# U and the read-out computed transposed, with two heads in two column halves, in an RWKV-7 plus SoLU kernel

## The chip, the cores and the metric

One core of one Trainium2 chip runs the whole program. The metric is the device time of one execution in microseconds (us); several runs are summed up by their median. Below, PE is TensorE (PEld its weight loads), DVE is VectorE, ACT is ScalarE, POOL is GpSimd, and SP is SyncE, which here only issues transfers.

## The reference, cut to what matters

A recurrence over 768 steps for 4 batches of 8 heads with 40 channels each, and behind it a two-layer MLP over the 3072 tokens:

```python
for t in range(S):
    y[:, :, t] = einsum('bhd,bhde->bhe', r_t, state)
    Sa = einsum('bhde,bhe->bhd', state, a_t)
    state = state * w_t[:, :, None, :] - einsum('bhd,bhe->bhde', Sa, b_t) \
            + einsum('bhd,bhe->bhde', v_t, k_t)
x = y.transpose(0, 2, 1, 3).reshape(3072, 320)
h = x @ w_in                       # 320 -> 1024
solu = h * softmax(h)
ln = (solu - mean) / sqrt(var + 1e-6) * g_ln
out = ln @ w_out                   # 1024 -> 320
```

All data are 32-bit floats, except the three MLP weights, which arrive as 64-bit floats and are narrowed on DVE.

## The kernel before

Time is cut into 6 chunks of 128 steps, which gives N = 24 (chunk, batch) pairs; a pass `i` handles one pair, with the batches in turn. `front(i)` (six passes ahead) makes the decay factors: `decay` takes the logarithm of `w`, sums it along time with products against constant triangles (`pcum`) and takes exponentials (`inv`, `ex`); POOL scales `k`, `b` and `a` with them (`kb`, `ah`), and PE transposes `ah` and `b` (`paT`, `pbT`) and multiplies them to the triangular matrix `nt`. `invert(n)` inverts the 32x32 diagonal blocks of four passes on DVE, and `solve` joins them to the inverse of the 128x128 triangle, `tinvT`, with small products (`py`, `pz`; 32x32 and 64x64). Results of `front` pass through DRAM (`aT_dram`, `kb_dram`, `nt_dram`) and come back by `bring(i)` as `aTx`, `kbx`, `ntx`. `attend` makes the masked score matrices `psi` and `lamv` (one 128x128 matrix for each head). `recurrence` forms `x0`, then U by eight products with `tinvT` (`pu`), the new state (`pst`), and the masked scores `lamu` from U transposed (`pnuT`). `readout` adds up y in `pyo`, scales it with `ex` into `x`, and transposes it into `xT` (`pxT`). `mlp(i - 2)` makes `h`, the softmax and the normalisation, transposes (`plnT`) and multiplies with the second weight (`po`).

The main loop writes a pass in two halves, each with `in_turn`, which takes one step of each part by turns: first `attend(i+1)`, `recurrence(i)` and `front(i+6)`, then `solve(i+1)`, `readout(i)` and `mlp(i-2)`. A scheduler orders the instructions of each engine from that; every engine, and SP's queue of transfers, runs its list strictly in order. A 32-bit matrix product in the source is two MATMUL instructions with a weight load each in the trace; a transpose is one. The read-out's products are

```python
for h in range(H):
    for j, lam in enumerate((d["lamv"], d["lamu"])):
        nc.tensor.matmul(t[:, h * D:h * D + D], lhsT=lam[:, h % 2, h // 2, :], rhs=kb[:, j, h, 0:D], ...)
```

that is, 128x128 weights are loaded for each and 40 columns stream through them.

Of the kernel before, what the change touches and what calls it, by code (L numbers as in the profile page):

```python
# [17 lines left out]
Q = 32  # L18
GRP = 4
# [32 lines left out]
def kernel(  # L52
# [28 lines left out]
    NK = -(-DM // P)  # L81
# [35 lines left out]
    ah_t = zeroed("ah", [P, H, 64], 2)  # L117
# [7 lines left out]
    x_t = zeroed("x", [P, NK * P], 2)  # L125
    y_mid = const.tile([P, 2, G, Q], FP32, name="y_mid")
    y_last = const.tile([P, 2, G, 64], FP32, name="y_last")
    w_in = zeroed("w_in", [P, NK, DFF], 1)[0]
# [32 lines left out]
    def load_weight(dst, src):  # L161

        if src.dtype == FP32:
            nc.scalar.dma_start(out=dst, in_=src)
            yield
            return
        n, width = src.shape
        for lo in range(0, width, 128):
            hi = min(width, lo + 128)
            bits = two.tile([P, 128], I64, tag="bits", name="bits")[0:n, 0:hi - lo]  # L170
            nc.scalar.dma_start(out=bits, in_=src[:, lo:hi])
            narrow(dst[:, lo:hi], bits)
            yield

    def weights():
        nc.scalar.dma_start(out=g_rows, in_=moe_g_ln.rearrange("(c p) -> c p", p=P))
        for kt in range(NK):
            n = min(P, DM - kt * P)
            yield from load_weight(w_in[0:n, kt, :], moe_w_in[kt * P:kt * P + n, :])
# [3 lines left out]
        for c in range(NF):  # L183
            yield from load_weight(w2[:, c, :], moe_w_out[c * P:(c + 1) * P, :])
# [3 lines left out]
    def rows(p):  # L188
        return slice(64 * p, 64 * p + 64)
# [16 lines left out]
    def scores(name, lhs, rhs, dst):  # L206

        for p in range(2):
            t = bank("p" + name)
            for g in range(G):  # L210
                nc.tensor.matmul(t[:, g * P:(g + 1) * P], lhsT=lhs[rows(p), g, :],  # L211
                                 rhs=rhs[rows(p), g, :], start=True, stop=True)
# [14 lines left out]
    def load(i, late=False):  # L227
# [13 lines left out]
        for n, ap in (("w", w), ("k", k), ("b", b), ("a", a)):  # L241
            d["raw_" + n] = raw.tile([P, H, D], FP32, tag="raw_" + n, name="raw_" + n)
            nc.sync.dma_start(out=d["raw_" + n], in_=src(ap))

    def decay(i):

        d = st[i]
        lw, kb, ah = lw_t[i % 2], kb_t[i % 2], ah_t[i % 2]
# [7 lines left out]
        t = bank("pcum")  # L256
# [8 lines left out]
        f = ex[:, DM:].rearrange("p (g f c) -> p g f c", g=G, f=2)  # L265
        d["to_mid"] = f[:, :, 1, :]
        d["to_end"] = small.tile([P, G, 2], FP32, tag="to_end", name="to_end", bufs=AHEAD + 1)
        nc.gpsimd.tensor_tensor(out=d["to_end"], in0=f[:, :, 0, :],
                                in1=c_("diag").rearrange("p (g c) -> p g c", c=2), op=ALU.mult)
        d["ah"] = ah  # L270

# [8 lines left out]
    def front(i):  # L280
# [12 lines left out]
        scores("nt", bT, aT, nt)  # L293
# [41 lines left out]
    def bring(i):  # L335
# [13 lines left out]
        d["aT"] = two.tile([P, G, P], FP32, tag="aTx", name="aTx")  # L349
        nc.sync.dma_start(out=d["aT"], in_=d["aT_dram"])  # L350
# [62 lines left out]
    def recurrence(i):  # L413
# [14 lines left out]
        x0 = two.tile([P, DM], FP32, tag="x0", name="x0")  # L428
        nc.scalar.copy(out=x0, in_=t[:, 0:DM])
# [177 lines left out]
```

## Time and profile before

| what | value |
|---|---|
| median of 3 runs | 1231.67 us (1228.69 to 1231.69) |
| the profiled execution's own time | 1226.91 us |
| its span, from first to last instruction | 1225.1 us |
| PE busy | 1111.7 us, 91% of the span |
| DVE, ACT, POOL busy | 522.2, 261.1, 133.2 us |
| mean granted clock of PE | 0.791 of full speed |

The stages below are cut where the first product `px` of `recurrence` starts in pass 0, pass 3 and pass 23 (157.4, 289.4 and 1158.2 us). The profiled execution took 1.8 us more than its span and 4.8 us less than the median. The clock that the profile shows for PE has two levels, 1.2 and 2.4 GHz; a mean of 0.50 over a stretch says that all of it ran at the lower one, 1.00 that all ran at the higher. An instruction's duration includes its way through the array, so neighbours overlap; the pace of a group is read from the chain of waits, where a group's time over its count is the step from one to the next.

### The profile page before, as it was taken

The page shows a single profiled execution, that of the slowest core. Times are in us where ns is not written, and L with a number is a line of the kernel's source. Part 1 is how long each engine was busy: PE and PEld are TensorE (multiplying, and loading weights), DVE is VectorE, ACT ScalarE, POOL GpSimd, SP SyncE. Part 2 cuts the span into 40 slices and gives each one's busy share as a digit, 9 for nine tenths or more (in the row PEclk, how much of TensorE's full clock was granted, in tenths as well). Part 3 has the DMA queues.
Part 4 walks back from the last instruction along what each step waited for, and adds up shares of the span by engine and source line. Part 5 has one row for each costly group of instructions (what it writes and reads, how often), then busy time and mean ns, then how long its engine had stood idle before and what let it go on. Part 6 is the DMA issues. An engine that isn't in the chain of part 4 may idle for free.

```text
span 1225.1 us, 20360 instructions
## 1 busy us (share of the span) xinstructions
PE 1111.7 (91%) x8281; PEld 904.7 (74%) x8281; DVE 522.2 (43%) x1466; ACT 261.1 (21%) x549; POOL 133.2 (11%) x182
## 2 busy tenths in 40 slices
PE   1753499999899999999999999999999999999986
PEld 1642397888698878788788788788788778788763
DVE  5779932275223373132552242562233743331222
ACT  1211021123123212122212122222222212122111
POOL 6210013001011001011001011001101000000000
PEclk9855566588689877789768789889888888788777
DMA  9656542443343333253234243235223122210000
GB/s 158 151 125 167 141 99 73 103 90 109 64 102 87 83 82 99 57 115 88 72 83 104 60 113 89 71 83 132 76 54 94 33 74 60 47 36 6 6 6 11
DMA packets 275740, 101.22 MB, mean 83 GB/s; under 512 B 250680, under 2 KB 259392, under 8 KB 275648
## 3 DMA queue, kind: packets, MB, share of 16 engines
q1 hardware_dynamic: 269088, 94.41, 33.1%
q10 hardware_dynamic: 6560, 5.52, 1.7%
q8 instruction: 65, 1.06, 0.4%
q14 instruction: 27, 0.22, 0.1%
HBM read 62.14 MB, written 37.75 MB: 82 GB/s over the span
## 4 chain that ended last, share of the span: by engine, by line
PE 85%; DVE 7%; DMA 3%; issue 2%; ACT 1%; POOL 1%; SPq 0%; POOLq 0%; DVEq 0%; ACTq 0%
PE h L489 15%; PE pyo L469 9%; PE po L526 9%; PE pz L380 4%; PE pu L433 4%; PE pst L441 4%; PE plamv L211 4%; PE px L426 3%; PE py L400 3%; PE pz L407 3%; PE ppsi L211 3%; PE plamu L211 3%; PE pnt L211 2%; PE plnT L521 2%; PE py L380 2%
## 5 line engine op out<-in xcount | busy, mean ns | idle before, releaser
L489 PE MATMUL h<-w_in,xT 128*128 128x512 f32 x288 | 205.5, 838 | 7.8 <-DVE c L508 7.8
L526 PE MATMUL po<-w,lnT 128*128 128x320 f32 x384 | 110.5, 442 | 0.0
L526 PEld LDWEIGHTS po<-w,lnT 128*128 128x128 f32 x384 | 75.3, 197 | 40.8 <-issue 8.0
L489 PEld LDWEIGHTS h<-w_in,xT 128*128 128x128 f32 x288 | 67.0, 265 | 51.7 <-issue 49.0
L213 DVE TENSOR_TENSOR psi<-ppsi,cst 128x512 f32<-128x512 f32 x48 | 31.5, 686 | 172.9 <-PE ppsi L211 172.9
L469 PE MATMUL pyo<-kbx,lamu 128*128 128x40 f32 x384 | 92.2, 331 | 0.0
L469 PE MATMUL pyo<-kbx,lamv 128*128 128x40 f32 x384 | 89.3, 323 | 0.0
L469 PEld LDWEIGHTS pyo<-kbx,lamu 128*128 128x128 f32 x384 | 75.2, 243 | 1.0 <-issue 1.0
L469 PEld LDWEIGHTS pyo<-kbx,lamv 128*128 128x128 f32 x384 | 72.7, 236 | 0.2
L493 DVE TENSOR_REDUCE nmax<-h 128x1 f32<-128x1024 f32 x24 | 29.4, 1224 | 90.5 <-PE h L489 90.5
L211 PE MATMUL pnt<-aT,bT 64*128 64x128 f32 x384 | 52.0, 335 | 16.9 <-ACT bT L203 16.9
L324 DVE TENSOR_TENSOR u<-u,prod 128x30 f32<-128x30 f32 (+9 forms) x180 | 60.2, 335 | 4.0
L473 DVE TENSOR_TENSOR x<-pyo,ex 128x320 f32<-128x320 f32 x24 | 11.8, 492 | 117.5 <-PE pyo L469 117.5
L322 DVE TENSOR_TENSOR prod<-blk,u 128x30 f32<-128x30 f32 (+9 forms) x180 | 60.0, 334 | 4.2
L409 DVE TENSOR_SCALAR tinvT<-pz 64x256 f32<-64x256 f32 x48 | 19.9, 416 | 96.7 <-PE pz L407 96.2
L511 POOL TENSOR_TENSOR rs<-c,mhalf 128x1 f32<-128x1 f32 x24 | 13.4, 560 | 436.2 <-DVE c L510 397.5
L211 PEld LDWEIGHTS pnt<-aT,bT 64*128 64x128 f32 x384 | 46.7, 233 | 19.2 <-ACT bT L203 19.2
L380 PE MATMUL py<-tinv,ntx 32*32 32x32 f32 x768 | 27.8, 196 | 34.9 <-DMA tinv<-ut_dram 34.9
L213 DVE TENSOR_TENSOR lamv<-plamv,cst 128x512 f32<-128x512 f32 x48 | 31.7, 687 | 64.7 <-PE plamv L211 64.7
L400 PEld LDWEIGHTS py<-tinv,ntx 64*64 64x64 f32 x384 | 39.7, 206 | 24.8 <-issue 18.3
L211 PEld LDWEIGHTS plamu<-rT,nuT 64*128 64x128 f32 x384 | 39.5, 200 | 21.9 <-ACT nuT L203 21.9
L263 POOL TENSOR_TENSOR kb<-raw_k,inv 128x320 f32<-128x320 f32 x24 | 20.9, 871 | 319.8 <-ACT inv L255 303.5
(122 smaller groups left out, 2011.8 us busy)
## 6 DMA issues: line engine op xcount, KB each, us to landing
kb_dram<-kb SPq DMA_DIRECT2D x24, 512.0 KB, 3.3
kbx<-kb_dram SPq DMA_DIRECT2D x24, 512.0 KB, 4.0
aT_dram<-aT SPq DMA_DIRECT2D x24, 256.0 KB, 2.3
aTx<-aT_dram SPq DMA_DIRECT2D x24, 256.0 KB, 3.0
nt_dram<-nt SPq DMA_DIRECT2D x24, 192.0 KB, 2.8
ntx<-nt_dram SPq DMA_DIRECT2D x24, 192.0 KB, 3.0
raw_w<-in_w_dram SPq DMA_DIRECT2D x24, 160.0 KB, 3.5
raw_k<-in_k_dram SPq DMA_DIRECT2D x24, 160.0 KB, 3.6
```

The source lines that it names most:

```text
L211: nc.tensor.matmul(t[:, g * P:(g + 1) * P], lhsT=lhs[rows(p), g, :], rhs=rhs[rows(p), g, :], start=True, stop=True)
L213: nc.vector.tensor_tensor(out=dst[:, p], in0=t.rearrange("q (g c) -> q g c", g=G), in1=tri.unsqueeze(1).to_broadcast([P, G, P]), op=ALU.mult)
L322: nc.vector.tensor_tensor(out=t, in0=nb[:, j:j + 1, j + 1:Q].to_broadcast([P, j, m]), in1=u[:, 0:j, j:j + 1].to_broadcast([P, j, m]), op=A ...
L324: nc.vector.tensor_tensor(out=u[:, 0:j, j + 1:Q], in0=u[:, 0:j, j + 1:Q], in1=t, op=ALU.subtract)
L380: nc.tensor.matmul(t[quarter(out), c:c + Q], lhsT=lhs(p, g), rhs=rhs(p, g), start=True, stop=True)
L400: nc.tensor.matmul(t[hi, g * 64:g * 64 + 64], lhsT=nt[lo, G * p + g, 32:96], rhs=tinv[lo, p, g, :], start=True, stop=True)
L407: nc.tensor.matmul(t[lo, g * 64:g * 64 + 64], lhsT=y_last[hi, p, g, :], rhs=tinvT[hi, p, g, hi], start=True, stop=True)
L433: nc.tensor.matmul(t[:, h * D:h * D + D], lhsT=d["tinvT"][:, h % 2, h // 2, :], rhs=x0[:, h * D:h * D + D], start=True, stop=True)
L441: nc.tensor.matmul(t[:, g * 80:g * 80 + 80], lhsT=pair(kb[:, j], g), rhs=x[:, 2 * g:2 * g + 2, 0:D], start=j == 0, stop=j == 1)
L469: nc.tensor.matmul(t[:, h * D:h * D + D], lhsT=lam[:, h % 2, h // 2, :], rhs=kb[:, j, h, 0:D], start=not ci and h == 0 and j == 0, stop=j ...
L489: nc.tensor.matmul(h[:, hh], lhsT=d["xT"][:, kt, :], rhs=w_in[:, kt, hh], start=kt == 0, stop=kt == NK - 1)
L526: nc.tensor.matmul(o[:, 0:DM], lhsT=lnT[:, f, :], rhs=w2[:, f, :], start=f == 0, stop=f == NF - 1)
```

## The change

- **U transposed.** `pu` swaps its operands: `x0` of a head (128x64, padded) is loaded as weights and `tinvT` of the head (128 columns) streams. Even heads write output partitions 0 to 63, odd heads 64 to 127 of the same bank. The result is U transposed (`nuT`) at once; U itself comes from four transposes back (`pnu`).
- **Read-out transposed.** `pyo` swaps its operands in the same way: `kb` of a head (128x64) is loaded, the score matrix (128 columns) streams, two heads in two column halves. y comes out as channels by time; DVE scales it with the factors `exT` (128x512 instead of 128x320), and four transfers from SBUF to SBUF pack 40 of each 64 rows into `xT`. The three transposes `pxT` and the ACT copy behind them are gone.
- **Factors transposed.** `decay` makes the factors for `a` transposed (`pcx`: 4 products with 132 columns, two exponentials) instead of one product with 320 columns and four with 4; `a` is transposed raw and scaled by DVE out of PSUM (`ax`), so that POOL's `ah` and ACT's copy of `aT` are gone. `ax` with the factors (520 KB) goes through DRAM instead of `aT` (256 KB); `to_end` is made in `bring`.
- **MLP split.** `mlp` becomes `hidden` (up to the normalised `ln`), written beside `recurrence` in the first half of a pass, and `output` in the second.
- **Weights.** `w_in` is cut into tiles of 3, 3 and 2 heads, so that each block of its narrowing is fetched by three (two) transfers on ACT's queue instead of one; the zero fill of `w_in` on POOL is gone.

```diff
-        ex = d["ex"] = two.tile([P, DM + 16], FP32, tag="ex", name="ex", bufs=AHEAD + 1)
+        ax = d["ax"] = two.tile([P, G, AXW], FP32, tag="ax", name="ax")
...
-        nc.tensor.matmul(t[:, 0:DM], lhsT=c_("cum_ex"), rhs=lw[:, :, 0:D], start=True, stop=True)
-        for g in range(G):
-            nc.tensor.matmul(t[:, DM + 4 * g:DM + 4 * g + 4], lhsT=pair(lw, g), rhs=c_("half"),
-                             start=True, stop=True)
-        nc.scalar.activation(out=ex, in_=t[:, 0:DM + 16], func=AF.Exp)
+        for j in range(2):
+            t = bank("pcx")
+            for g in range(2):
+                nc.tensor.matmul(t[:, g * 132:g * 132 + 132], lhsT=pair(lw, 2 * j + g), rhs=cst[:, lo:lo + 132],
+                                 start=True, stop=True)
+            nc.scalar.activation(out=ax[:, 2 * j:2 * j + 2, P:], in_=t[:, 0:264].rearrange("p (g t) -> p g t", g=2),
+                                 func=AF.Exp)
...
-        nc.gpsimd.tensor_tensor(out=ah[:, :, 0:D], in0=d["raw_a"], in1=heads(ex[:, 0:DM]), op=ALU.mult)
...
-        aT = transposed("aT", d["ah"], "aT", 2)
+        t = bank("paT")
+        for g in range(G):
+            nc.tensor.transpose(out=t[:, g * P:(g + 1) * P], in_=pair(d["a"], g), identity=ident)
+        nc.vector.tensor_tensor(out=ax[:, :, 0:P], in0=t.rearrange("p (g t) -> p g t", g=G), in1=ax[:, :, P:2 * P],
+                                op=ALU.mult)
...
         t = bank("pu")
         for h in range(H):
-            nc.tensor.matmul(t[:, h * D:h * D + D], lhsT=d["tinvT"][:, h % 2, h // 2, :],
-                             rhs=x0[:, h * D:h * D + D], start=True, stop=True)
-        nc.scalar.mul(out=nu[:, :, 0:D], in_=heads(t[:, 0:DM]), mul=-1.0)
+            nc.tensor.matmul(t[half(h % 2), h // 2 * P:h // 2 * P + P], lhsT=x0[:, h, :],
+                             rhs=d["tinvT"][:, h % 2, h // 2, :], start=True, stop=True)
+        nuT = two.tile([P, G, P], FP32, tag="nuT", name="nuT")
+        nc.scalar.mul(out=nuT.rearrange("p g t -> p (g t)"), in_=t, mul=-1.0)
+        yield
+        t = bank("pnu")
+        for g in range(G):
+            nc.tensor.transpose(out=t[:, g * P:(g + 1) * P], in_=nuT[:, g, :], identity=ident)
+        nc.scalar.copy(out=nu.rearrange("p h c -> p (h c)"), in_=t)
...
-                nc.tensor.matmul(t[:, h * D:h * D + D], lhsT=lam[:, h % 2, h // 2, :], rhs=kb[:, j, h, 0:D],
-                                 start=not ci and h == 0 and j == 0, stop=j == 1, skip_group_check=True)
+                nc.tensor.matmul(t[half(h % 2), h // 2 * P:h // 2 * P + P], lhsT=kb[:, j, h, :],
+                                 rhs=lam[:, h % 2, h // 2, :], start=not ci and h < 2 and j == 0, stop=j == 1,
+                                 skip_group_check=True)
...
-        x = x_t[i % 2]
-        nc.vector.tensor_tensor(out=x[:, 0:DM], in0=t[:, 0:DM], in1=d["ex"][:, 0:DM], op=ALU.mult)
-        yield
-        t = bank("pxT")
-        for kt in range(NK):
-            nc.tensor.transpose(out=t[:, kt * P:(kt + 1) * P], in_=x[:, kt * P:(kt + 1) * P], identity=ident)
-        d["xT"] = two.tile([P, NK, P], FP32, tag="xT", name="xT", bufs=LAG + 2)
-        nc.scalar.copy(out=d["xT"].rearrange("p k t -> p (k t)"), in_=t[:, 0:NK * P])
+        x = two.tile([P, G, P], FP32, tag="x", name="x")
+        nc.vector.tensor_tensor(out=x, in0=t.rearrange("p (g t) -> p g t", g=G), in1=d["exT"], op=ALU.mult)
+        xT = d["xT"] = two.tile([P, NK, P], FP32, tag="xT", name="xT", bufs=LAG + 1)
+        for p in range(2):
+            nc.sync.dma_start(out=xT[p * D:p * D + D], in_=x[64 * p:64 * p + D, 0:3, :])
+            nc.sync.dma_start(out=xT[2 * D:3 * D, p, :], in_=x[64 * p:64 * p + D, 3, :])
...
-        in_turn(*([attend(i + 1)] if more else []), *([recurrence(i)] if i < N else []), ...
-                *([some(ws, 4, 3)] if i < LAG else []))
+        in_turn(*([attend(i + 1)] if more else []), *([recurrence(i)] if i < N else []), ...
+                *([hidden(i - LAG)] if i >= LAG else []), *([some(ws, 4, 3)] if i < LAG else []))
...
-                *([mlp(i - LAG)] if i >= LAG else []), *([some(inv, 8)] if inv else []),
+                *([output(i - LAG)] if i >= LAG else []), *([some(inv, 8)] if inv else []),
```

The scheduler moves more than the diff shows. On PE, from the end of the read-out of a middle pass to the start of the next pass's first transposes, before:

```order
L469 MATMUL pyo<-kbx,lamu 128x40
L489 MATMUL h<-w_in_128,xT 128x512
L380 MATMUL pz<-tinvT_92,y_mid 32x32 x16
L380 MATMUL pz<-y_mid,tinvT_92 32x32 x8
L400 MATMUL py<-tinv_96,ntx 64x64 x8
L477 MATMUL pxT<-cst,x_124 128x128 x3
L407 MATMUL pz<-tinvT_92,y_last 64x64 x8
L489 MATMUL h<-w_in_128,xT 128x512 x4
L521 MATMUL plnT<-cst,e 128x128 x8
L489 MATMUL h<-w_in_128,xT 128x512
L526 MATMUL po<-w_130,lnT 128x320 x8
L201 MATMUL pkT<-cst,kbx 128x128 x4
```

and the same place of the change:

```order
L485 MATMUL pyo<-lamu,kbx 64x128
L540 MATMUL plnT<-cst,e 128x128 x8
L392 MATMUL pz<-tinvT_94,y_mid 32x32 x16
L392 MATMUL pz<-y_mid,tinvT_94 32x32 x8
L545 MATMUL po<-w_129,lnT 128x320 x8
L412 MATMUL py<-tinv_98,ntx 64x64 x8
L504 MATMUL h<-w_in,xT 128x512
L419 MATMUL pz<-tinvT_94,y_last 64x64 x8
L504 MATMUL h<-w_in,xT 128x512 x2
L206 MATMUL pkT<-cst,kbx 128x128 x4
```

`po` moved from right ahead of `pkT` to the middle of the small products, and `plnT`, which needs DVE's finished `e`, right behind the read-out. On SP, whose list holds all transfers of the main loop, the place of the load of `kbx` (the next pass's `k` and `b`, which `pkT` reads first) in a middle pass, before:

```order
L300 DMA blk_dram<-nt 32x8x32 x4
L304 DMA nt_dram<-nt 512x1x96
L304 DMA nt_dram<-nt 256x1x32
L347 DMA tinvT_94<-u_dram 32x8x32 x3
L350 DMA aTx<-aT_dram 128x512
L352 DMA kbx<-kb_dram 128x1024
L239 DMA rv_104<-in_r_dram 128x8x40
L530 DMA out_dram<-osb 128x320
```

and in the change (the first two rows stand there twice, once for each half of the heads):

```order
L493 DMA xT<-x 40x384
L494 DMA xT<-x 40x128
L356 DMA axx<-ax_dram 128x1040
L549 DMA out_dram<-osb 128x320
L364 DMA kbx<-kb_dram 128x1024
L350 DMA ntx<-nt_dram 64x768
```

The load of `kbx` now stands behind the four transfers that pack y, and in 9 of the 15 passes from 3 to 17, as here, behind the store of the output, which waits for `po` and its copy `osb`; in 3 of these 9 four or more transfers of `tinvT` and `tinv` stand ahead of it as well. On DVE, between the maximum of `h` (`nmax`) and the end of the normalisation (the last row, which `plnT` needs), in a middle pass of the change:

```order
L508 TENSOR_REDUCE nmax<-h 128x1
L218 TENSOR_TENSOR lamv<-plamv,cst 128x512 x2
L513 TENSOR_TENSOR e<-h,e 128x1024
L218 TENSOR_TENSOR lamu<-plamu,cst 128x512 x2
L218 TENSOR_TENSOR nt<-pnt,cst 128x512
L517 BN_STATS bs<-e 128x6
...
L466 TENSOR_TENSOR tot<-pst,sm_120 128x320
...
L468 TENSOR_TENSOR st_116<-tot,to_end 128x8x40
L525 TENSOR_TENSOR c_5738<-c_5738,mv 128x1
L528 TENSOR_SCALAR e<-e,mv,rs 128x1024
L490 TENSOR_TENSOR x<-pyo,axx 128x512
```

The masks `lamv`, `lamu` and `nt` (a second row each of `nt` and `bs` and four small rows are left out) now stand among the MLP's steps; in many passes before, the steps of the MLP stood behind them.

## Rows read from the trace of the kernel before

**Rows 1.** The page's parts 1 and 4: busy times, and the chain by engine.

```profile
PE 1111.7 (91%) x8281; PEld 904.7 (74%) x8281; DVE 522.2 (43%) x1466; ACT 261.1 (21%) x549; POOL 133.2 (11%) x182
...
PE 85%; DVE 7%; DMA 3%; issue 2%; ACT 1%; POOL 1%; SPq 0%; POOLq 0%; DVEq 0%; ACTq 0%
```

**Rows 2.** Windows by stage: length, busy of each engine, PEclk, DMA share, GB/s.

```profile
0.00:157.40 157.40, 71.99 (x384) 61.71 (x385) 123.32 (x595) 21.47 (x43) 35.66 (x53) 0.66 0.68 148
157.40:289.40 132.00, 128.14 (x938) 110.60 (x937) 55.51 (x133) 26.49 (x59) 19.25 (x24) 0.69 0.36 85
289.40:1158.20 868.80, 861.18 (x6758) 697.06 (x6757) 326.61 (x711) 202.11 (x428) 76.69 (x102) 0.83 0.32 76
1158.20:1225.10 66.90, 50.37 (x206) 35.30 (x204) 16.73 (x30) 10.98 (x21) 1.64 (x3) 0.80 0.03 10
```

**Rows 3.** Windows, `pyo` alone: length, PE, PEld, DVE, PEclk, DMA share, GB/s.

```profile
307.50:321.10 13.60, 4.67 (x23) 4.52 (x22) 0.49 (x1) 0.50 0.28 47
399.70:403.10 3.40, 3.40 (x34) 3.40 (x32) 0.00 (x0) 1.00 0.45 83
403.10:413.40 10.30, 1.44 (x8) 1.29 (x7) 0.49 (x1) 0.50 0.48 133
...
1133.60:1140.40 6.80, 4.28 (x21) 4.13 (x20) 0.49 (x1) 0.50 0.00 0
```

**Rows 4.** The chain at full clock: start us, us, what, and how many.

```profile
413.30 1.12 PE pz L407 x16
...
415.45 0.86 PE h L489 x2
...
420.62 0.44 PE pkT L201 x4
...
425.15 0.54 PE pcum L257 x2
425.69 0.79 PE pcum L259 x8
...
428.11 1.91 PE pu L433 x16
...
440.01 1.05 PE pyo L464 x8
441.06 3.89 PE pyo L469 x32
```

**Rows 5.** Timeline of PE, products over 64 rows: start us, us, what.

```profile
395.49 1.38 PE L211 MATMUL plamu<-rT,nuT 64*128 64x128 f32 x13
396.60 0.37 PE L211 MATMUL pnt<-aT,bT 64*128 64x128 f32 x1
...
396.93 0.27 PE L211 MATMUL plamu<-rT,nuT 64*128 64x128 f32 x1
```

**Rows 6.** Timeline of PE and its weight loads in the read-out.

```profile
400.22 0.35 PE L469 MATMUL pyo<-kbx,lamv 128*128 128x40 f32 x2
400.37 0.30 PEld L469 LDWEIGHTS pyo<-kbx,lamu 128*128 128x128 f32 x2
```

**Rows 7.** The page's part 6: a DMA issue, KB, median us to landing.

```profile
kbx<-kb_dram SPq DMA_DIRECT2D x24, 512.0 KB, 4.0
```

**Rows 8.** Timeline of SP: the issue of that load in one pass.

```profile
404.57 0.35 SPq L352 DMA_DIRECT2D kbx<-kb_dram  x1
```

**Rows 9.** SP's own waits from 200 to 1100 us: total, times, longest.

```profile
SPq L530 <- ACT osb L528: 174.4, 16, 18.0
```

**Rows 10.** Waits over the whole span: us in total, times, longest.

```profile
DVE n_man L149 <- DMA bits<-in_moe_w_in_dram: 15.8, 9, 5.1
...
PE plnT L521 <- DVE e L513: 7.6, 2, 7.1
...
DVE w_in L159 <- POOL w_in L98: 7.0, 1, 7.0
```

**Rows 11.** The page's part 5, a mask on DVE.

```profile
L213 DVE TENSOR_TENSOR psi<-ppsi,cst 128x512 f32<-128x512 f32 x48 | 31.5, 686 | 172.9 <-PE ppsi L211 172.9
```

More of the change, by code (lines that the diff above doesn't have):

```diff
@@ L18 @@
 Q = 32
+TILE_HEADS = ((0, 1, 6), (2, 3, 7), (4, 5))
 GRP = 4
@@ L124 @@
     sm_t = zeroed("sm", [P, G, 2, 64], 2)
-    x_t = zeroed("x", [P, NK * P], 2)
+    x0_t = zeroed("x0", [P, H, 64], 2)
     y_mid = const.tile([P, 2, G, Q], FP32, name="y_mid")
     y_last = const.tile([P, 2, G, 64], FP32, name="y_last")
-    w_in = zeroed("w_in", [P, NK, DFF], 1)[0]
+    AXW = 2 * P + 4
+    w_in = const.tile([P, NK, DFF], FP32, name="w_in")
     w2 = const.tile([P, NF, DM], FP32, name="w2")
@@ L159, in narrow, with load_weight @@
         nc.vector.tensor_tensor(out=dst, in0=frac, in1=scale.bitcast(FP32), op=ALU.mult)
-    def load_weight(dst, src):
-        if src.dtype == FP32:
-            nc.scalar.dma_start(out=dst, in_=src)
-            yield
-            return
-        n, width = src.shape
+    def load_weight(dst, parts):
+        n, width = dst.shape
+        wide_ = parts[0].dtype != FP32
         for lo in range(0, width, 128):
             hi = min(width, lo + 128)
-            bits = two.tile([P, 128], I64, tag="bits", name="bits")[0:n, 0:hi - lo]
-            nc.scalar.dma_start(out=bits, in_=src[:, lo:hi])
-            narrow(dst[:, lo:hi], bits)
+            to = dst[:, lo:hi]
+            if wide_:
+                to = two.tile([P, 128], I64, tag="bits", name="bits")[0:n, 0:hi - lo]
+            row = 0
+            for part in parts:
+                nc.scalar.dma_start(out=to[row:row + part.shape[0]], in_=part[:, lo:hi])
+                row += part.shape[0]
+            if wide_:
+                narrow(dst[:, lo:hi], to)
             yield
@@ L177, in weights @@
         for kt in range(NK):
-            n = min(P, DM - kt * P)
-            yield from load_weight(w_in[0:n, kt, :], moe_w_in[kt * P:kt * P + n, :])
+            yield from load_weight(w_in[0:D * len(TILE_HEADS[kt]), kt, :],
+                                   [moe_w_in[h * D:h * D + D, :] for h in TILE_HEADS[kt]])
         pg = bank("pg")
@@ L183, in weights, with half @@
         for c in range(NF):
-            yield from load_weight(w2[:, c, :], moe_w_out[c * P:(c + 1) * P, :])
+            yield from load_weight(w2[:, c, :], [moe_w_out[c * P:(c + 1) * P, :]])
             nc.gpsimd.tensor_scalar(out=w2[:, c], in0=w2[:, c], scalar1=g_col[:, c:c + 1],
                                     scalar2=None, op0=ALU.mult)
-    def rows(p):
+    def half(p):
         return slice(64 * p, 64 * p + 64)
@@ L210, in scores @@
             for g in range(G):
-                nc.tensor.matmul(t[:, g * P:(g + 1) * P], lhsT=lhs[rows(p), g, :],
-                                 rhs=rhs[rows(p), g, :], start=True, stop=True)
+                nc.tensor.matmul(t[:, g * P:(g + 1) * P], lhsT=lhs[half(p), g, :],
+                                 rhs=rhs[half(p), g, 0:P], start=True, stop=True)
             nc.vector.tensor_tensor(
@@ L255, in decay @@
         nc.scalar.activation(out=inv, in_=t[:, 0:DM], func=AF.Exp)
-        t = bank("pcum")
-        nc.tensor.matmul(t[:, 0:DM], lhsT=c_("cum_ex"), rhs=lw[:, :, 0:D], start=True, stop=True)
-        for g in range(G):
-            nc.tensor.matmul(t[:, DM + 4 * g:DM + 4 * g + 4], lhsT=pair(lw, g), rhs=c_("half"),
-                             start=True, stop=True)
-        nc.scalar.activation(out=ex, in_=t[:, 0:DM + 16], func=AF.Exp)
+        lo = where["cum_ex"][0]
+        for j in range(2):
[5 more added lines that the diff above has]
+                                 func=AF.Exp)
         for j, n in enumerate("kb"):
             nc.gpsimd.tensor_tensor(out=kb[:, j, :, 0:D], in0=d["raw_" + n], in1=heads(inv), op=ALU.mult)
-        nc.gpsimd.tensor_tensor(out=ah[:, :, 0:D], in0=d["raw_a"], in1=heads(ex[:, 0:DM]), op=ALU.mult)
[L265 to L270, printed above, removed]
     def quarter(q):
@@ L348, in bring @@
                               in_=u[homes(i, q)].rearrange("h s t -> s h t"))
-        d["aT"] = two.tile([P, G, P], FP32, tag="aTx", name="aTx")
-        nc.sync.dma_start(out=d["aT"], in_=d["aT_dram"])
+        ax = d["ax"] = two.tile([P, G, AXW], FP32, tag="axx", name="axx")
+        nc.sync.dma_start(out=ax, in_=d["ax_dram"])
+        d["aT"], d["exT"] = ax[:, :, 0:P], ax[:, :, P:2 * P]
+        f = ax[:, :, 2 * P:].rearrange("p g (f c) -> p g f c", f=2)
+        d["to_mid"] = f[:, :, 1, :]
+        d["to_end"] = small.tile([P, G, 2], FP32, tag="to_end", name="to_end")
+        nc.gpsimd.tensor_tensor(out=d["to_end"], in0=f[:, :, 0, :],
+                                in1=c_("diag").rearrange("p (g c) -> p g c", c=2), op=ALU.mult)
         d["kb"] = two.tile([P, 2, H, 64], FP32, tag="kbx", name="kbx")
@@ L427, in recurrence @@
                              start=not ci and h == 0, stop=True, skip_group_check=True)
-        x0 = two.tile([P, DM], FP32, tag="x0", name="x0")
-        nc.scalar.copy(out=x0, in_=t[:, 0:DM])
+        x0 = x0_t[i % 2]
+        nc.scalar.copy(out=x0[:, :, 0:D], in_=heads(t[:, 0:DM]))
         yield
@@ L488, in mlp @@
             for kt in range(NK):
-                nc.tensor.matmul(h[:, hh], lhsT=d["xT"][:, kt, :], rhs=w_in[:, kt, hh],
+                n = len(TILE_HEADS[kt]) * D
+                nc.tensor.matmul(h[:, hh], lhsT=d["xT"][0:n, kt, :], rhs=w_in[0:n, kt, hh],
                                  start=kt == 0, stop=kt == NK - 1)
-        yield
+            yield
         nmax = small.tile([P, 1], FP32, tag="nmax", name="nmax")
@@ L511, in mlp, with output @@
         nc.gpsimd.tensor_tensor(out=rs, in0=c2, in1=mhalf, op=ALU.pow)
-        ln = q
+        ln = d["ln"] = q
         nc.vector.tensor_scalar(out=ln, in0=q, scalar1=mv[:, 0:1], scalar2=rs, op0=ALU.subtract, op1=ALU.mult)
         yield
-        yield
+    def output(i):
+        d = st[i]
+        bi, ci = where_(i)
+        ln = d["ln"]
         lnT = two.tile([P, NF, P], FP32, tag="lnT", name="lnT", bufs=1)
```

29 lines of the change are left out of this document (14 added, 15 removed).

## The prediction

> **What bounds the kernel now.** I read the shares of the engines and the chain first: PE is busy for 91% of the span and carries 85% of the chain; no other engine reaches half [rows 1]. So PE's own time counts, not that of POOL, ACT or DVE, as long as they keep ahead. Then the windows by stage [rows 2]. Until the first `px` at 157.4 us PE is busy for 72 us and DVE for 123 (it narrows weights): DVE bounds that stage. In the three passes after it, in the 20 passes from 289.4 to 1158.2 and in most of the tail PE bounds; in the 20 passes it is busy for 861.2 of 868.8 us, so a pass takes 43.4 us and PE hardly waits.
>
> But the granted clock of that stage is 0.83 of full: with two levels, 34% of its time runs at half clock. The windows around the read-out say where [rows 3]: from 399.7 to 403.1 us the clock is 1.00 and PE does nothing but `pyo`; then it is 0.50 for 10.3 us, into the small products behind. Read in this way, 20 of the 27 stretches at half clock that begin from 289.4 to 1158.2 us begin while the read-out's products run or within 0.5 us of their end; the first and the last of the 27 are shown. The read-out is also PE's longest piece of small products in a pass: 32 of them in 3.89 us, a pace of 0.12 us for 40 columns, where a transpose of 128 columns paces at 0.11 [rows 4]. So the 128x128 weight load sets the pace and the array idles between; this is the work behind which the clock falls.
>
> **The change part by part**, per pass, at full clock. A pass of 43.4 us at 0.83 is 36.1 us at full clock (a half-clock microsecond counts half).
>
> *Read-out and U.* 32 and 16 instructions remain, now with 128 columns streaming and half the weights. No row shows two column halves of one bank with all 128 rows. Bounds: with no overlap they stream at 0.11 us each, 3.52 and 1.76 us; with the halves fully side by side, one step more than half the count, 17 and 9 steps, 1.87 and 0.99. The nearest row is the score products over 64 rows, where two row halves alternate: the first `pnt` starts at 396.60 while `plamu` of the other half still starts products until 396.93 [rows 5], so queued work of two halves does run side by side. I take the second: 3.89 to 1.87 and 1.91 to 0.99, together -2.94 (with no overlap -0.52).
>
> *Product with the state.* 8 instructions, 1.05 us; with 128 columns 8 x 0.11 = 0.88: -0.17. *`pxT`*: three transposes, -0.33. *Factors*: `pcum` of L257 and L259, 0.54 + 0.79, become 8 instructions of 132 columns, 0.88: -0.45 [rows 4]. U's four transposes remain. Sum: -3.89, to 32.2 us; without overlap -1.47, to 34.6.
>
> *DVE* gets `ax` (0.69, as a mask [rows 11]) and a wider `x`, about 0.9 us on the 16.3 that it works in a pass (326.6 over 20 [rows 2]); it stays far below PE. ACT loses two copies and gets an exponential, POOL loses `ah`: hidden behind PE, at nothing; if the cover were gone, ACT's 10.1 us and POOL's 3.8 a pass would still fit three times over.
>
> *Changes of shape.* Two more stretches of half-width products make four more switches of PE's shape a pass. A switch can cost between nothing and the 0.27 us that a product takes to run through [rows 5], so 0 to 1.1; I take 0.3, since the chain shows no gap at the switches that are there. The Trainium skill (TensorEngine Tiling (Array Packing), Key Properties) says that a change of tiling mode drains the engine, which speaks against this change; it gives no price, and by the upper bound above the sum would be 0.8 a pass higher.
>
> *`kbx` on SP.* Its load is now queued behind the packing of y and, in 9 of 15 passes, behind the store of the output. SP already spends its longest waits on that store, 174 us in 16 waits [rows 9], but elsewhere. From the end of `po` to `pkT` PE has two small groups of 1.12 and two or three `h` products of 0.86 [rows 4], 4.0 to 4.8 us. The load needs `po`'s copy (at most a mask's 0.69), two issues of 0.35 and 4.0 to land [rows 7, 8, 11]: 5.4. So PE waits 0.6 to 1.4 us in six of the 15, some 2 us more in the three with `tinvT` and `tinv` ahead, and `pvT`, `prT`, `px` and all else of PE queue behind it: on average 0.9 to 1.3 over 15; I take 1.0.
>
> *The MLP's split.* `plnT` waited for DVE only twice [rows 10]. Now six masks and the state's two sums stand among the MLP's steps on DVE, and `plnT` directly behind `pyo`. Bound: nothing to six masks, 4.1 us; I take 0.5, since about ten PE groups lie between `nmax` and `plnT`.
>
> *The clock.* With 128 columns streaming, the read-out has the density of the stretch from `po` to `psi`, behind which the clock did not fall. Bounds: all falls go (0 us), or one of 10.3 us stays in each pass (5.2 lost). I take a fall in every sixth pass, 0.8, from the waits above and the INV work on DVE.
>
> A pass: 32.2 + 0.3 + 1.0 + 0.5 + 0.8 = 34.8, 20 passes 696 (before 868.8). The first three: 132 at 0.69 is 91 at full clock, less 3 x 3.9 is 79; DVE still narrows there and the clock has to come back, the upper bound is 132 - 12 = 120; I take 100. Start: 157, bounds 150 to 167: DVE no longer waits 7.0 us for the zero fill [rows 10], but three transfers instead of one feed each of 16 blocks (two for 8 more); DVE already waited for the single ones. Tail: 66.9 at 0.80 is 53.5 at best; I take 58. Span 157 + 100 + 696 + 58 = 1011. The profiled execution lies 1.8 above its span and 4.8 below the median, so the forecast is **1018 us**, its own range 975 to 1060.
>
> **Rivals.**
> - *No overlap of the column halves* (0.13). For it: no row shows them. Clock back, but 2.4 more a pass; DVE then has time, -0.5: 1018 + 20 x 1.9 + 3 x 2.4 = 1063.
> - *Load and product in turn* (0.04). If half-width loads could not run behind a product in the same rows, an instruction would cost its 0.11 and about 0.055 of load: 48 x 0.165 = 7.9 against 2.86, +5.1 a pass: 1018 + 23 x 5.1 - 10 = 1125. Against it: a load starts at 400.37 while the products of the head before, over the same 128 rows, run until 400.57 [rows 6]. The Trainium skill (TensorE: Matmul & The Clock Gate, Part 3, The mechanism) states just this rule, that loads overlap products in flight only in other row groups; this trace disagrees, by that pace of 0.12.
> - *The clock goes on falling in every pass* (0.13), since the small products behind stay: a loss of 5.2 to 6.8 (half of 10.3 and 13.6 [rows 3]) instead of 0.8, 20 x 4.4 to 6.0 and about 10 in the first passes: 1115 to 1148, say 1130.
> - *`kbx` late in every pass* (0.07): 3.4 instead of 1.0, 1018 + 20 x 2.4 = 1066, and 1100 where the clock falls on the wait.
> - *Slower* (0.04): `po` and `h` no longer stand in one dense piece; in the trace the clock rises where they do. If it stays low, a pass of 34.0 us of work takes 34.0 / (1 - s/2) with a share s at half clock; it passes 43.4 at s = 0.43 (now 0.34), and at 0.6 takes 48.6: 1018 + 20 x 13.8 = 1294.
> - *No effect* (0.01): the gain in PE turns into other waits of the same size, 1225 to 1235.
>
> **How the numbers follow.** The forecast has 0.58. The range that should hold 8 in 10 leaves out the slower case, no effect, the upper half of the falling clock, half of the loads in turn and the forecast's own low end, where every unknown term is zero (below 955): **955 to 1125**. A measurement here can tell about 0.3%. Only the last two rivals are not faster: faster 0.95, same 0.01, slower 0.04.
>
> **What the new profile would show.** Right: PEclk of the passes above 0.95; no fall behind `pyo`; `pyo`'s 32 products in 1.9 us and `pu`'s 16 in 1.0; PE still over 90% busy; passes of some 35 us. Wrong, and where: 3.5 us for `pyo` means no overlap, 5 us loads in turn; PEclk near 0.83 means that the small products hold the clock down; waits of PE `pkT` for `kbx` or of `plnT` for DVE above 1 us a pass mean that the order on SP or DVE bounds; a start above 170 us means the split fetch of `w_in`.

## The result and the profile after

The changed kernel takes 1007.04 us (1005.14 to 1008.71, 4 runs), a ratio of 0.8176 to the kernel before with an interval of 0.8151 to 0.8201; 1018 was forecast. The profiled execution took 1006.36 us, with a span of 1004.5. Executions over 1.5% longer than the fastest of the same kernel count in no ratio below, among them one of run 3 that took 1488.9 us at a mean granted clock of 0.605.

Parts 1 and 4 of the page of the changed kernel answer to [rows 1]:

```profile
PE 879.2 (88%) x8161; PEld 699.6 (70%) x8161; DVE 534.6 (53%) x1490; ACT 248.3 (25%) x525; POOL 108.1 (11%) x157
...
PE 79%; DVE 9%; DMA 7%; issue 2%; SPq 1%; ACT 0%; ACTq 0%; POOLq 0%; DVEq 0%
```

The windows by stage of the changed kernel, cut at the first `px` of passes 0, 3 and 23 like [rows 2] (length, busy time and count of PE, PEld, DVE, ACT and POOL, PEclk, DMA share, GB/s):

```profile
0.00:151.90 151.90, 61.00 (x372) 53.13 (x373) 126.50 (x594) 19.43 (x42) 27.70 (x42) 0.69 0.70 166
151.90:260.60 108.70, 99.95 (x932) 77.18 (x932) 60.26 (x151) 25.51 (x57) 18.23 (x21) 0.88 0.55 136
260.60:945.90 685.30, 674.66 (x6653) 541.42 (x6651) 330.63 (x716) 193.00 (x409) 60.53 (x91) 0.99 0.44 113
945.90:1004.50 58.60, 43.60 (x209) 27.83 (x208) 17.18 (x32) 10.40 (x19) 1.64 (x3) 0.91 0.03 12
```

The span is 220.6 us shorter: 5.5 in the start, 23.3 in the first three passes, 183.5 in the 20 passes, 8.3 in the tail. A pass went from 43.4 to 34.3 us. If a microsecond at half clock counts half, the clock cost 868.8 x (1 - 0.83) = 148 us in the 20 passes before and 685.3 x (1 - 0.99) = 7 now: some 141 of the 183.5 us. Part of the work loses less than half at half clock, by about 0.4 us a pass (shown below), so an estimate is 133 us from the clock and the other 50, 2.5 a pass, from less work on PE.

The chain through one pass at full clock (start us, us, what, count):

```profile
529.33 0.89 PE pyo L481 x8
530.22 1.95 PE pyo L485 x32
532.17 1.02 PE plnT L540 x8
533.19 1.43 PE pz L392 x48
534.62 4.50 PE po L545 x16
539.13 1.07 PE py L412 x16
...
548.78 0.90 PE pcx L267 x8
...
551.32 1.02 PE pu L445 x16
552.34 0.59 PE paT L289 x4
552.93 0.44 PE pbT L206 x4
...
556.73 0.59 PE pnu L452 x4
```

Against [rows 4] the read-out's 32 products fell from 3.89 to 1.95 us and U's 16 from 1.91 to 1.02: their two column halves run side by side. `paT` and `pnu`, groups of four transposes like `pbT`, take 0.15 us more than it: they stand directly behind products in halves.

PE's waits in the 20 passes, and DVE's for weights in the start (us in total, times, longest), which answer to [rows 10]; `issue` says that the profile names nothing that PE waited for:

```profile
PE h L504 <- issue: 6.6, 2, 3.9
PE pkT L206 <- DMA kbx<-kb_dram: 3.9, 3, 2.0
```

```profile
DVE n_man L151 <- DMA bits<-in_moe_w_in_dram: 15.3, 7, 8.1
DVE n_man L151 <- DMA bits<-in_moe_w_out_dram: 4.7, 5, 1.2
```

Two falls of the clock are left in the 20 passes, where there were 27, and each begins during one of PE's two waits in front of `h`. The second, in the chain, on DVE's timeline and in the window behind:

```profile
395.99 2.79 PE h L504 x6
398.78 3.85 issue
402.62 5.18 PE h L504 x6
```

```profile
401.30 1.22 DVE L513 TENSOR_TENSOR e<-h,e 128x1024 f32<-128x1024 f32 x1 [1.27 <-ACT e L511]
```

```profile
400.60:407.40 6.80, 4.78 (x6) 2.06 (x7) 3.76 (x8) 0.66 (x2) 0.55 (x1) 0.50 0.48 131
```

`h` has one buffer in PSUM, the memory that PE writes to. The next pass's `h` starts at 402.62, as DVE's product `e`, which reads the last one, ends (401.30 + 1.22); meanwhile PE stands still, and at 400.6 the clock falls. The first wait reads the same: `e` ends at 360.31 and `h` starts at 360.41. That `h` waits for its buffer is read from these times. PE's two longer waits for `kbx`, of 1.7 and 2.0 us, were not followed by a fall.

### The profile page after: what moved, and what is told of

Same layout as the page of the kernel before. It is cut to its first block, busy times and chain, and to the rows that moved or that the text cites. A ratio compares the mean times of both kernels' runs of the same rounds, so it can differ in the third digit from the quotient of the medians.

```text
span 1004.5 us, 20445 instructions
## 1 busy us (share of the span) xinstructions
PE 879.2 (88%) x8161; PEld 699.6 (70%) x8161; DVE 534.6 (53%) x1490; ACT 248.3 (25%) x525; POOL 108.1 (11%) x157
## 4 chain that ended last, share of the span: by engine, by line
PE 79%; DVE 9%; DMA 7%; issue 2%; SPq 1%; ACT 0%; ACTq 0%; POOLq 0%; DVEq 0%
PE h L504 13%; PE po L545 11%; PE pyo L485 5%; PE px L438 4%; PE pst L461 4%; PE plamv L216 4%; PE ppsi L216 4%; PE plamu L216 3%; PE pz L392 3%; PE pnt L216 3%; DMA kbx<-kb_dram 3%; DMA bits<-in_moe_w_in_dram 3%; PE plnT L540 3%; PE pu L445 2%; PE py L392 2%
## 5 line engine op out<-in xcount | busy, mean ns | idle before, releaser
L504 PE MATMUL h<-w_in,xT 120*128 120x512 f32 (+1 forms) x288 | 157.2, 666 | 18.2 <-issue 18.2
L504 PEld LDWEIGHTS h<-w_in,xT 120*128 120x128 f32 (+1 forms) x288 | 52.5, 205 | 61.7 <-issue 58.1
L216 PE MATMUL pnt<-ax,bT 64*128 64x128 f32 x384 | 46.8, 311 | 27.1 <-ACT bT L208 14.6
L216 PEld LDWEIGHTS pnt<-ax,bT 64*128 64x128 f32 x384 | 41.8, 210 | 28.7 <-ACT bT L208 28.7
L438 PE MATMUL px<-rv,psi 128*128 128x40 f32 x384 | 47.4, 285 | 0.0
L438 PEld LDWEIGHTS px<-rv,psi 128*128 128x128 f32 x384 | 46.5, 198 | 0.0
L216 PEld LDWEIGHTS plamv<-rT,vT 64*128 64x128 f32 x384 | 37.9, 193 | 9.2 <-issue 8.4
L216 PE MATMUL plamv<-rT,vT 64*128 64x128 f32 x384 | 42.6, 291 | 0.0
L216 PE MATMUL ppsi<-axx,kT 64*128 64x128 f32 x384 | 42.4, 291 | 0.0
L511 ACT ACTIVATE e<-h,nmax 128x1024 f32<-128x1024 f32 x24 | 26.9, 1121 | 62.4 <-DVE nmax L508 62.4
```

Source lines behind the costliest of these rows:

```text
L216: nc.tensor.matmul(t[:, g * P:(g + 1) * P], lhsT=lhs[half(p), g, :], rhs=rhs[half(p), g, 0:P], start=True, stop=True)
L438: nc.tensor.matmul(t[:, h * D:h * D + D], lhsT=d["psi"][:, h % 2, h // 2, :], rhs=vb[:, h, 0:D], start=not ci and h == 0, stop=True, skip_ ...
L504: nc.tensor.matmul(h[:, hh], lhsT=d["xT"][0:n, kt, :], rhs=w_in[0:n, kt, hh], start=kt == 0, stop=kt == NK - 1)
```

## The experiments

The theory at the outset was that of the prediction: halves that alternate run side by side, and the clock came back because the read-out streams 128 columns instead of 40. The main rival: it came back because the split put `plnT` and `po` behind the read-out. Each ratio here is to the kernel before as measured again beside the run (medians of 1224.5 us for runs 1 to 4, 1221.7 for 5 to 8 and 1222.3 for 9 to 12), so it isn't to be set beside the 0.8176 above.

**1. Halves in turn.** The even heads first, then the odd ones, all else in the same order:

```diff
-        for h in range(H):
+        for h in (0, 2, 4, 6, 1, 3, 5, 7):
```

> The changed kernel with the 32 products of the read-out written for the four even heads first and the four odd heads behind them, so that the two column halves of the array no longer alternate; the order of everything else is the same. Theory (halves that alternate run side by side): the 32 products go from 1.95 to about 3.5 us a pass, +1.6 x 24 = 38, so 1045 us, with the clock of the passes still near 0.99, since 128 columns stream through in every step. Rival A (half as many weight columns are loaded in half the time and that alone sets the pace): still 1.95 us, 1007 us. Rival B (the clock holds only because both halves are filled): the clock falls behind the read-out in each pass, 1007 + 38 + 20 x 5 = 1145 us.

1043.68 us (ratio 0.857, 0.8496 to 0.8645). Its chain:

```profile
579.65 0.89 PE pyo L481 x8
580.54 3.26 PE pyo L485 x32
```

3.26 against 1.95 us for the same products: 1.31 x 24 = 31 of the 37 us; the rest is about what four falls of the clock in the 20 passes instead of two cost. The alternation makes the overlap; half as many weight columns without it bring at most a third of the gain (3.26 against the 3.89 of [rows 4]).

**2. The old operands in the 32 products.**

```diff
+        n = D if ci else 64
...
-                nc.tensor.matmul(t[half(h % 2), h // 2 * P:h // 2 * P + P], lhsT=kb[:, j, h, :],
-                                 rhs=lam[:, h % 2, h // 2, :], start=not ci and h < 2 and j == 0, stop=j == 1,
-                                 skip_group_check=True)
+                nc.tensor.matmul(t[:, h * 64:h * 64 + n], lhsT=lam[:, h % 2, h // 2, :], rhs=kb[:, j, h, 0:n],
+                                 start=not ci and h == 0 and j == 0, stop=j == 1, skip_group_check=True)
```

> The changed kernel with the old operand order in the read-out alone: the 128x128 scores are loaded, 40 columns of kb stream (64 in the first four passes), so that y is put in the wrong layout and the output is not the reference's. Theory (the read-out's few columns pulled the clock down): 32 products take 3.5 to 3.9 us again, +1.75 x 24 = 42, and the clock falls behind the read-out in nearly each of the 20 passes, 3.4 to 6.8 us lost each time: 1120 to 1185 us, granted clock of the passes 0.83 to 0.88. Rival (the clock came back since po and h moved in among the small products): 1007 + 42 = 1049 us, granted clock above 0.96.

1042.70 us (0.8545, 0.8461 to 0.8628): the rival's number. Its chain:

```profile
583.83 1.09 PE pyo L481 x8
584.92 3.50 PE pyo L486 x32
588.42 0.90 PE plnT L540 x8
```

The read-out's 32 products are as thin as before for 3.50 us, and the clock holds: three falls in the 20 passes. The first half of the theory, that the read-out's 40 columns by themselves pull the clock down, is wrong.

**3. The new operands with few columns.** 40 of the 128 columns stream (`n`) from the fifth pass on:

```diff
+        n = D if ci else P
...
-                nc.tensor.matmul(t[half(h % 2), h // 2 * P:h // 2 * P + P], lhsT=kb[:, j, h, :],
-                                 rhs=lam[:, h % 2, h // 2, :], start=not ci and h < 2 and j == 0, stop=j == 1,
+                nc.tensor.matmul(t[half(h % 2), h // 2 * P:h // 2 * P + n], lhsT=kb[:, j, h, :],
+                                 rhs=lam[:, h % 2, h // 2, 0:n], start=not ci and h < 2 and j == 0, stop=j == 1,
```

> The changed kernel in which the read-out's products stream 40 of the 128 columns of the scores from the fifth pass on; weights, halves and count are those of the change. The other columns of y get only the product with the state, so the output is not the reference's. Theory (columns streaming hold the clock): the 32 products take at most 1.95 us, but the clock falls behind the read-out in most passes: 1007 + 20 x 3.4 to 6.8 = 1075 to 1145 us. Rival (operand order and weights of 64 columns are what matters): no new falls, 1000 to 1007 us. If the pace goes below 1.95 us, columns set it; if it stays, the weight loads do.

980.41 us (0.805, 0.7955 to 0.8146), below both expectations, with no fall in the 20 passes:

```profile
589.64 1.08 PE pyo L486 x32
590.73 1.02 PE plnT L541 x8
```

1.08 instead of 1.95 us: with half-width weights and 128 columns the columns set the pace, not the weight loads. With 40 they no longer do alone: 40/128 of 1.95 would be 0.61. What sets the 1.08 isn't shown. And in this trace 1.08 us of thin work did no harm to the clock.

**4. The MLP in one piece** in the second half of a pass, with the yields of before:

```diff
...
-                *([hidden(i - LAG)] if i >= LAG else []), *([some(ws, 4, 3)] if i < LAG else []))
+                *([some(ws, 4, 3)] if i < LAG else []))
...
-                *([output(i - LAG)] if i >= LAG else []), *([some(inv, 8)] if inv else []),
+                *([mlp(i - LAG)] if i >= LAG else []), *([some(inv, 8)] if inv else []),
```

> The changed kernel with the MLP in one piece again in the second half of a pass, with the yields it had before. Theory (the split brings nothing on PE's path; read-out and U do): 997 to 1017 us, granted clock of the passes above 0.95, kbx late in fewer passes since po stands nearer to pkT or in more, within 0.5 us a pass. Rival (po among the small products is what holds the clock): falls behind the small products in each pass, 1007 + 20 x 3.4 to 5 = 1075 to 1107 us.

1004.33 us (0.8251, 0.818 to 0.8323), six falls. So the split isn't needed either: the rival falls with this run, as the theory fell with the second. Without the split the 20 passes take 697.3 us, 12 more than in the changed kernel, and the three before them 95.7, 13 fewer, so its gain and its loss cancel. `pkT` waited for `kbx` once in the 20 passes, for 2.6 us.

**5 to 7. One part alone, and both taken back.** In the kernel before, the read-out alone (its 32 products and the product with the state) and the split alone; in the changed kernel, edits 2 and 4 together.

> The kernel before with the read-out and the product with the state transposed and nothing else; x is still taken from the old layout, so the output is not the reference's. Theory 1 (the read-out's dense stretch by itself is enough for the clock, though the rest of a pass stays as before): 2.1 us a pass from the pairs and most of the falls gone, granted clock of the 20 passes above 0.95, 1040 to 1090 us. Theory 2 (what holds the clock in the changed kernel is that plnT and po stand behind the read-out, as the run with the old operands suggests): only the pairs, 24 x 2.1 / 0.83 = 61 less, 1160 to 1180 us, clock near 0.83.

> The kernel before with the MLP split over the slot and nothing else. Theory 1 (only the read-out's density counts): the falls stay, 1215 to 1245 us. Theory 2 (dense work directly behind the read-out is enough, whatever the read-out's own products): the clock of the 20 passes goes from 0.83 to above 0.95, a pass from 43.4 to 37 or 38 us, 1100 to 1140 us.

> The changed kernel with both taken back: the old operand order in the read-out (40 columns stream, output not the reference's, as in the run with the old operands) and the MLP in one piece in the second half. Theory 3 (either of the two is enough, so that only without both the clock falls): falls behind the read-out in most passes, granted clock of the 20 passes 0.83 to 0.90, 1043 + 20 x 3 to 6 = 1100 to 1160 us. Rival (the other parts, U, the factors and the lost pxT, hold the clock): 1035 to 1055 us, clock above 0.95.

1091.92 us (0.8969, 0.8897 to 0.9041), 1170.53 us (0.9611, 0.9524 to 0.9698) and 1112.93 us (0.9153, 0.9072 to 0.9235). The window of the 20 passes in each, in this order, and behind them those of runs 2 and 4:

```profile
278.00:1028.10 750.10, 742.01 (x6760) 602.72 (x6759) 323.42 (x711) 201.66 (x428) 75.84 (x102) 0.94 0.37 88
```

```profile
287.40:1102.90 815.50, 805.36 (x6750) 661.09 (x6748) 323.89 (x707) 203.07 (x429) 75.21 (x102) 0.90 0.34 81
```

```profile
253.50:1045.10 791.60, 779.51 (x6665) 637.65 (x6664) 343.57 (x718) 194.73 (x408) 61.17 (x91) 0.89 0.39 99
```

```profile
267.70:978.70 711.00, 708.47 (x6653) 581.79 (x6651) 336.90 (x716) 192.92 (x410) 63.69 (x91) 0.98 0.43 109
```

```profile
245.80:943.10 697.30, 687.85 (x6663) 555.95 (x6662) 341.45 (x718) 192.88 (x408) 61.22 (x91) 0.97 0.44 112
```

The read-out alone comes out just above theory 1's range, both taken back within theory 3's. In the kernel before, the read-out by itself brings the clock of the passes from 0.83 to 0.94, the split by itself to 0.90; neither expectation for the split alone was met, it lies between them. In the changed kernel the 32 products and the split can each be taken back alone (0.98, 0.97); without both the clock goes back to 0.89. The way from there to 0.83 belongs to the parts that run 7 leaves in. The split alone hardly makes falls rarer, 22 instead of 27, but shorter, 171 us at half clock instead of 297: in its chain, behind a fall at 903.4 us, `po` follows, and the stretch at half clock ends at 910.2.

```profile
903.15 1.43 PE plnT L526 x8
904.58 2.32 PE pz L380 x48
906.90 6.15 PE po L531 x16
```

```profile
903.40:910.20 6.80, 6.80 (x61) 5.23 (x60) 1.11 (x3) 1.54 (x3) 0.00 (x0) 0.50 0.38 98
```

**8. Wider blocks of weights**, to see what sets the start:

```diff
...
-        for lo in range(0, width, 128):
-            hi = min(width, lo + 128)
+        for lo in range(0, width, 160):
+            hi = min(width, lo + 160)
...
```

> The changed kernel with the weights narrowed in blocks of 160 columns instead of 128 (37 blocks instead of 48, two temporaries used again to make room). If DVE bounds the start, 11 blocks x 11 steps x about 0.1 us of fixed cost = 12 us less before the first px: 993 to 998 us. If the fetches of the weights bound it: 1003 to 1010 us.

1003.72 us (1001.58 to 1007.44; 0.8241, 0.8185 to 0.8297), not to be told from the changed kernel. The first `px` comes 5.6 us earlier, where 12 were expected:

```profile
0.00:146.30 146.30, 58.83 (x373) 51.11 (x374) 125.98 (x494) 19.96 (x43) 27.59 (x42) 0.71 0.74 174
```

DVE works as long as before (126.0 against 126.5 us) with 100 instructions fewer, and its waits for weights fell from 20.0 to 11.3 us: what was saved is waiting, not work. The fixed cost of an instruction was overrated.

**9 and 10. Further back from run 2.** The product with the state in the old order too (DVE's product `x` then takes 40 of each 64 columns), and, in another kernel, U in the old order too (its four transposes then stand in front of the scores):

```diff
-                nc.tensor.matmul(t[:, g * P:g * P + P], lhsT=d["sT"][:, g, :], rhs=d["rT"][:, g, :],
+                nc.tensor.matmul(t.rearrange("p (g c d) -> p g c d", g=G, c=2)[:, g, :, 0:D], lhsT=d["rT"][:, g, :],
+                                 rhs=d["sT"][:, g, :].rearrange("p (c d) -> p c d", c=2)[:, :, 0:D],
...
```

```diff
-            nc.tensor.matmul(t[half(h % 2), h // 2 * P:h // 2 * P + P], lhsT=x0[:, h, :],
-                             rhs=d["tinvT"][:, h % 2, h // 2, :], start=True, stop=True)
+            nc.tensor.matmul(t[:, h * 64:h * 64 + D], lhsT=d["tinvT"][:, h % 2, h // 2, :], rhs=x0[:, h, 0:D],
+                             start=True, stop=True)
...
```

> The changed kernel with the whole read-out in the old operand order: besides the 32 products of the run with the old operands also the product with the state, which streams 80 columns of the state instead of 128 of rT. The split of the MLP stays; the output is not the reference's. Theory 4 (the product with the state and the read-out are one stretch, and its columns, with what follows, decide the clock): falls come back in most of the 20 passes, but short ones, since plnT and po follow, as in the kernel before with the split: 1043 + 20 x 2 to 4.5 = 1083 to 1133 us. Rival (the other parts, U and the factors, hold the clock): 1035 to 1050 us with at most 4 falls.

> The run with the old operands, and U in the old operand order too (tinvT is loaded, 40 columns of x0 stream, U is transposed back as before). Theory 4 (U stands some 10 us ahead of the read-out and does not matter for its clock): pu 1.02 to 1.9 us, two steps of ACT as before, 0.9 x 24 = 21 more than 1043, so 1058 to 1068 us, with at most 5 falls in the 20 passes. Rival (U's denser products hold the clock): 1090 us and more.

1100.47 us (0.8911, 0.8786 to 0.9036) with 12 falls, and 1086.33 us (0.8861, 0.8781 to 0.8941) with 8, where run 2 had three. The first is theory 4's number: eight products with 80 columns instead of 128, right ahead of thin work, bring falls back, though at 10 us each they aren't short as expected. The second isn't theory 4's, and lies just below its rival's. Of its 2.4 us a pass over run 2 (759.6 against 711.0 in 20 passes), 0.9 are `pu` itself and 0.6 a new wait of PE, as the transposes of U now go through ACT before the scores:

```profile
PE plamu L216 <- ACT nuT L208: 11.1, 16, 0.8
```

The rest is falls at the read-out's end, though U stands some ten us ahead of it. Whether U's own products or only the moved place of the read-out in time makes them, these runs don't tell.

The trace of run 5 shows a second thin place. Four of its 11 falls begin while U's old products `pu` run, right behind `ppsi`, and they make 55 of its 92 us at half clock. One of them, in the chain and in the window behind (`pu` alone):

```profile
470.35 2.45 PE pu L433 x16
```

```profile
471.50:485.20 13.70, 1.30 (x7) 1.15 (x6) 0.44 (x1) 0.50 0.48 102
```

Two of the 27 falls of the kernel before and four of run 6's 22 begin there too, but none in the 20 passes of the changed kernel or of any run made from it, run 10 with its old U included. What those kernels have there, and run 5 lacks, is the new factors and, but for run 10, the new U. No run takes the factors back, so which of the two keeps the clock up there stays open.

**11 and 12. Wider blocks with a later split (FROM = 4), and the changed kernel again.**

```diff
...
-                *([hidden(i - LAG)] if i >= LAG else []), *([some(ws, 4, 3)] if i < LAG else []))
+                *([hidden(i - LAG)] if i >= FROM else []), *([some(ws, 4, 3)] if i < LAG else []))
...
-                *([output(i - LAG)] if i >= LAG else []), *([some(inv, 8)] if inv else []),
+                *([(output if i >= FROM else mlp)(i - LAG)] if i >= LAG else []), *([some(inv, 8)] if inv else []),
```

> A version from what the runs show: the wider blocks of the weights, the MLP in one piece in the passes 2 and 3 and split from pass 4 on. The first three passes took 95.7 us without the split and 108.7 with it (kbx waited behind the packing of y in pass 0), the 20 passes 697.3 without and 685.3 with it. If both hold together: 1004 - 12 = 988 to 995 us. If the first passes are set by DVE's weights, which the wider blocks moved too: 998 to 1005 us.

> The changed kernel once more, unchanged, beside the three others on the same chip: 1003 to 1010 us.

1009.15 us (0.8249, 0.8182 to 0.8316), above both expectations, and 1005.61 us (0.8227, 0.8145 to 0.831), as expected. The first three passes took 102.0 us, 6.7 fewer than in the changed kernel, but the 20 passes 697.4 where it has 685.3. No version that computes the whole output beats the changed kernel by more than the measurement can tell.

## Why the prediction was right, point by point

The time lies in the forecast's own range, by the mechanisms that it named. That it lies within 11 us is partly luck: the terms below were mis-sized by up to 0.8 us a pass and nearly cancel, as do the stages (start -5, first three passes +9, the 20 passes -11), and the median lay 2.5 us above the span where 6.6 were taken. One sign of being right did not show: PE is busy for 88% of the span, not over 90%; in the 20 passes it is 98%.

| us a pass (products from the chain above, waits and clock as means of the 20) | forecast | measured |
|---|---|---|
| read-out's 32 products | 1.87 | 1.95 |
| U's 16 products | 0.99 | 1.02 |
| product with the state | 0.88 | 0.89 |
| factors `pcx` | 0.88 | 0.90 |
| changes of shape | 0.3 | 0.5 |
| wait for `kbx` | 1.0 | 0.2 |
| wait of `plnT` for DVE | 0.5 | 0 |
| wait of `h` for its buffer | none | 0.3 |
| clock | 0.8 | 0.3 |
| a pass | 34.8 | 34.3 |

*Read-out and U*: right in mechanism and size; run 1 shows that the overlap comes from the alternation. *Load and product in turn* was rightly given 0.04: it asks for 0.165 us an instruction, and even with the halves in turn the pace is 3.26 / 32 = 0.10. The Trainium skill (TensorE: Matmul & The Clock Gate, Part 3, The mechanism) says in its list that loads overlap products in flight only where the row groups differ; a sentence above the list also allows a background buffer for weights. The list is contradicted again: in run 3 all 128 rows are used and an instruction takes 0.034 us, while its load is recorded with 0.14.

*The base*: "a half-clock microsecond counts half" was too kind. In the chain of the kernel before, inside and around a half-clock stretch:

```profile
884.53 0.46 PE paT L201 x4
...
889.45 0.44 PE pnuT L201 x4
...
899.95 2.32 PE pz L380 x48
...
904.28 1.90 PE py L400 x16
...
911.53 4.31 PE po L526 x16
```

```profile
898.10:908.30 10.20, 10.20 (x80) 7.27 (x79) 2.68 (x8) 1.59 (x4) 0.55 (x1) 0.50 0.34 84
```

`pz` takes 2.32 us at half clock and 1.43 at full, `py` 1.90 and 1.07: halved, they were counted 0.4 us a pass too short. *Changes of shape* cost 0.13 at `paT`, 0.15 at `pnu` (beside `pnuT`) and 0.19 at `po`, which now stands behind `pz`: 0.5 in place of 0.3. The Trainium skill (TensorEngine Tiling (Array Packing), Key Properties) says that such a change drains the engine; these rows agree, and give the price that it lacks. The first four rows of the table came out 0.1 longer, and the factors' saving of 0.45 was taken in all 20 passes though `front` runs in 15 of them, which is another 0.1. So PE's own work is 32.2 + 0.4 + 0.5 + 0.2 = 33.3; with waits and clock 34.1 of the 34.3 are explained, and 0.2 stay open.

*`kbx`*: the step that failed is its cover. (Its terms add up to 0.8 to 1.2 us, not 0.9 to 1.3, and that is a mean over 15 of the 20 passes.) Where the load stands right behind the store of the output, as in this chain, four or five products `h` (two instructions each) lie between `po` and `pkT`, not two or three:

```profile
503.94 1.07 PE py L412 x16
505.01 1.05 PE h L504 x2
506.07 1.07 PE pz L419 x16
507.14 3.64 PE h L504 x8
510.78 0.44 PE pkT L206 x4
```

That is 6.8 us from the end of `po`, not 4.0 to 4.8, and more than the 5.4 that the load was counted with. Apart from one wait of 0.3 us, PE waits in two passes, for 1.7 and 2.0 us, in which transfers of `tinvT` and of `axx` stand between the store and the load; the load itself took 4.4 us to land, where 4.0 were taken:

```profile
578.37 4.40 DMA kbx<-kb_dram
```

*The MLP's split* was priced as a risk alone; its gain, dense work directly behind the read-out, was not seen (12 us in the 20 passes, by run 4). *`h`'s buffer* was not thought of; its two waits are what is left of the falls.

*The clock*: that nearly all of it comes back was right, the reason only in part. Run 5 confirms that most of the loss went with the old read-out, its 32 products and the product with the state together (0.83 to 0.94). But the 32 products are not the cause by themselves (run 2: 0.98), nor is the split (run 4: 0.97). And the stretch from `po` to `psi` was misread as one behind which the clock did not fall: two of the 27 falls begin in `pu`, right behind `ppsi`. What the runs bear out is a looser statement: in a pass the thin work from the 32x32 products of `py` over the read-out to those of `pz` stands together, and the clock falls where enough of it does; denser read-out products, a product with the state of 128 columns and `plnT` with `po` in between each thin it out. Why run 10 loses part of the clock, and what the new factors do for it, stays open.

*Start*: 151.9 instead of 157. The wait of 7.0 us for the zero fill is gone, and the split fetch cost DVE 20.0 us of waits instead of 18.3. *First three passes*: 108.7 instead of 100; two waits of PE of 3.8 us for the buffer of `h` and, in pass 0, `kbx` behind the packing of y were missed.

## What to carry to other kernels

Where 128x128 weights are loaded to stream 40 columns, swap the operands: half-width weights in two alternating column halves gave 1.95 us for 3.89, and 3.26 where they did not alternate. Look up the granted clock by stretch before pricing a change of TensorE's work: here it was some 133 of the 183.5 us gained in the 20 passes. When several edits each thin out the same stretch, their gains don't add up; take each back alone from the final kernel, and all together, before one is named as the cause.

## What was not expected of the hardware

Products with weights of 64 columns, halves alternating, took 0.034 us each with 40 columns streaming (32 in 1.08 us) and 0.061 with 128 (32 in 1.95); 128x128 weights held 40 columns at 0.109 (32 in 3.50). PE waits of 2.8 and 3.9 us in a dense stretch of the changed kernel each had the clock fall, for 6.8 us at half clock: an estimate of 3.4 us lost, about as much again as the wait.
